# The second warming group ahead of the first turns of g, with a new instruction order: a convolution-and-FFN kernel on one core

## The chip, the cores and the metric

The kernel runs on one core of one Trainium2 chip. The metric is the device time of one execution in microseconds. The core's engines work side by side, each through its own list of instructions in order: TensorE (PE, matrix products), VectorE (DVE), ScalarE (ACT), GpSimd (POOL), and SyncE (SP), which issues DMA transfers. They wait for each other through semaphores. Some transfers are issued by ACT and POOL too. PE writes its results to PSUM, of which this kernel uses four tiles (`ps`), and DVE or ACT copy them out.

## What is computed

Two layers follow each other on 2048 positions of width 640: a long convolution with gates (H3), then a SwiGLU feed-forward network (FFN).

```python
def _A_ref(q, k, v, shift_k, ssm_k, ssm_D):
    ...                      # k_shift: four shifted copies of k times taps shift_k, added
    kv = k_shift * v
    ...                      # y: causal convolution of kv with ssm_k along the sequence, by FFT
    y = y + kv * ssm_D[None, None, :]
    return q * y

def _B_ref(x, w_gate, w_up, w_down):
    g = _silu(x @ w_gate)
    u = x @ w_up
    return (g * u) @ w_down

x = A_q
h = x + _A_ref(_layernorm(x, axis=-1), A_k, A_v, A_shift_k, A_ssm_k, A_ssm_D)
h2 = h + _B_ref(_layernorm(h, axis=-1), B_w_gate, B_w_up, B_w_down)
return h2
```

All inputs and the output are bfloat16. The FFN is 1728 wide.

## The kernel before

**Tiling.** The sequence is cut into four blocks of 512. In each block the stages are, by the names that the code gives them: `g` turns the block of ssm_k (positions to partitions; "turn" is a transpose, on PE against an identity, or by DMA), `G` is its spectrum (products with the cosine table WF, line 347), `k` makes kv from k, v and the taps (line 565, with a table `diag` of taps on diagonals), `X` is the spectrum of kv, `m` multiplies spectra and adds them up (lines 601 to 620: DVE products and sums, of which some sums are done by an adding DMA that POOL issues, line 255), `n` and `i` are the norm's statistics and the inverse transform (lines 677 to 742, products at 725), `t` normalises the result and turns it into `hT`, and `f` is the FFN: gate and up products (line 829), the SiLU and copies on ACT (818, 820), their product on DVE (823), and the down product (886). f of one block stands in the order beside the convolution of the next.

**The first microseconds.** SP issues the loads of ssm_k (g), k, the table WF, q (x), and so on; ACT issues the load of the taps (line 916); POOL issues that of the D row (961) and makes the identity (917). PE runs two warming groups (line 927), 18 and 16 products of ones that nobody reads, and between them, in the order of the code, four small products that turn the taps (934). DVE copies the taps (938), and DVE and POOL fill `diag` (945). Each block of g has four turns of five products (line 426), each copied out of PSUM (428); D's row is added to the first (430). For k the same stands at lines 528 and 532.

**What sets the order.** Every operation is recorded once with a number, an engine, what it reads and writes, and the operations it depends on (`deps`). `ORDER` is a list of these numbers; the program is written out in that order, so each engine gets its operations as they stand there. A number n below zero means operation ~n (46 for -47) in its other form, mostly the other engine: a copy on DVE instead of ACT, a fill of `diag` on POOL instead of DVE, a sum by DMA, a weight load issued by POOL instead of SP. Tiles are handed out along the order too, so the buffer numbers change with it. `schedule` refuses an order in which an operation stands ahead of one that it depends on.

**The dependences that matter here.** The turns of the taps depend on the first warming group, the second warming group on the turns of the taps, and the turns of k (`turned_k`) on the second warming group (`spun`, argument `behind`). The turns of g depend on g and the identity alone.

Of the kernel before, what the change touches and what calls it, by code (L numbers as in the profile page):

```python
# [41 lines left out]
TW = PAD + BLK  # L42
CUTS = ("X0", "G0", "m", "i")
ORDER = [
# [40 lines left out]
SLOTS = {'S': 8, 'big': 13, 'kT': 0, 'tT': 1, 'row': 5, 'sg': 0, 'co': 2, 'ps': 4, 'sm': 6}  # L85
HOME = {t: "big" for t in ("scr", "x", "ld", "t4", "hT", "wgu", "diag")} | {"o": "row", "ps_c": "ps", "ps_f": "ps"}
SPLIT = ((0,), (1,))
# [101 lines left out]
def kernel(ctx: ExitStack, tc: tile.TileContext, A_q, A_k, A_v, A_shift_k, A_ssm_k, A_ssm_D, B_x,  # L189
# [19 lines left out]
    def new(tag):  # L209
        return Buf(HOME.get(tag, tag), None, tag)  # L210
# [4 lines left out]
    def fixed(shp, dt, name):  # L215
        return Buf(None, const.tile(shp, dt, name=name))
# [7 lines left out]
    def pe(ns, fn, r, w, holds=(), late=338):  # L224
        op = plan.add("pe", ns, fn, r, w, holds)
        op.late = late
        return op
# [49 lines left out]
    ident = fixed([P, P], BF16, "ident")  # L277
# [127 lines left out]
            dve(wide(1490, ws), hi4, [odd, (dst, bits((0,), ws=ws))], [(dst, bits((1,), ws=ws))])  # L405
            sum_into(1490, lo4, lambda: ap(dst)[:, 0], lambda odd=odd: ap(odd), [odd], [(dst, bits((0,)))])

    def g_turned(g, drow=None):
        gT = new("t4")
        if plan.block in GTURN:  # L410
            by_r = new("scr")
            act(2350, lambda: nc.scalar.copy(ap(by_r).rearrange("q a b -> q (a b)").rearrange("q (r c p) -> q r c p", r=R, c=KT),
                                             ap(g).rearrange("q (c p r) -> q r c p", c=KT, r=R)), [g], [by_r], [gT])
            for r in range(R):
                def turned_by(q, r=r):
                    return lambda: q.dma_start(out=ap(gT)[:, r, :].rearrange("p (c q) -> p c q", c=KT),
                                               in_=ap(by_r).rearrange("q a b -> q (a b)")[:, r * D:(r + 1) * D], transpose=True)
                transfer(MB / 4, turned_by(nc.sync), [by_r], [(gT, r)])
            return gT
        for r in range(R):  # L420
            pt = conv_ps()

            def tr(r=r, pt=pt):
                src = ap(g).rearrange("q (c p r) -> q c p r", c=KT, r=R)
                for c in range(KT):
                    nc.tensor.transpose(turned(pt)[:, c * P:(c + 1) * P], src[:, c, :, r], ap(ident))  # L426
            pe(285, tr, [g, ident], [pt], [gT], 258)
            evict(lambda copy, r=r, pt=pt: copy(ap(gT)[:, r, :], turned(pt)[:, 0:D]), [pt], [(gT, r)], other=490)
        if drow:
            dve(480, lambda: nc.vector.tensor_add(ap(gT)[0:1, 0, :], ap(gT)[0:1, 0, :], ap(drow)[0:1, :]), [drow], [(gT, 0)])  # L430
        return gT
# [497 lines left out]
    spun = spin(WARMUP[0])  # L929
    pt = new("ps_c")  # L930
# [5 lines left out]
    spun = spin(WARMUP[1])  # L936
# [21 lines left out]
    g = load_g(0)  # L958
    first("Ld")
    drow = new("row")  # L960
# [5 lines left out]
    turned_k(k, spun, table)  # L966
    kv = kv_of(0, v)
    first("g0")
    gT = g_turned(g, drow)
    first("X0")  # L970
    X = [spectrum(kv, "X0", split("X0"))]
    first("G0")
# [12 lines left out]
    for j in range(1, NB):  # L985
# [3 lines left out]
        g = load_g(j)  # L989
# [12 lines left out]
        gT = g_turned(g)  # L1002
# [69 lines left out]
```

## Time and profile before

| what | us |
| --- | --- |
| median of three runs (lowest, highest) | 259.57 (258.88, 260.34) |
| the profiled execution's own time | 260.01 |
| its span, from the first to the last instruction | 258.3 |
| PE, DVE, ACT and POOL busy | 249.9, 193.4, 167.6, 54.6 |
| 540 products of line 829 (gate, up), busy | 120.3 |
| 416 products of line 886 (down), busy | 60.1 |
| 240 products of line 347 (spectra), busy | 38.7 |

An engine is busy while an instruction of its own runs. In the lists of waits a row reads "engine, line, waited for: us in total, times, longest". In the chain of work each row has its start, its length and the work that the end of the kernel hung on at that time. A row of the timeline has start, length, engine, line, operation, output and inputs, how many instructions were merged into it, and in brackets the idle time ahead of it and what ended it.

### The profile page before, as it was taken

How to read it: one execution, taken by the hardware profiler on the slowest of the kernel's cores; microseconds unless marked ns; L12 is line 12 of the kernel's file. 1: busy time of each engine (PE TensorE's matmuls, PEld its weight loads, DVE VectorE, ACT ScalarE, POOL GpSimd, SP SyncE). 2: the span in 40 equal slices, each digit the busy share in tenths (PEclk: the TensorE clock that was granted, in tenths of full speed). 3: DMA queues.
4: the chain of work that ended last, by engine and by line, in shares of the span. 5: the costliest groups of instructions: out<-in, count | busy, mean ns of one | idle time of the engine just before them, and what ended most of it. 6: DMA issues, size and time to landing. Idle time of an engine off the chain costs nothing.

```text
span 258.3 us, 5214 instructions
## 1 busy us (share of the span) xinstructions
PE 249.9 (97%) x2102; PEld 150.9 (58%) x2102; DVE 193.4 (75%) x306; ACT 167.6 (65%) x286; POOL 54.6 (21%) x70
## 2 busy tenths in 40 slices
PE   4999999999999999999999999999999999999994
PEld 3876777854545577744455577544447764444672
DVE  0599999999999899999998999998899300012222
ACT  2599999999898996765876783353497234434400
POOL 2750120122300211044431511039300022000000
PEclk9999999999999999999999999999999999999999
DMA  6993899999979598989999785658990336000003
GB/s 202 404 346 87 223 224 140 296 240 252 190 159 336 171 153 165 168 143 268 204 215 193 115 237 108 129 101 175 223 236 5 63 59 84 0 0 3 0 0 102
DMA packets 48034, 41.45 MB, mean 160 GB/s; under 512 B 25445, under 2 KB 41514, under 8 KB 48010
## 3 DMA queue, kind: packets, MB, share of 16 engines
q1 hardware_dynamic: 40368, 24.57, 36.4%
q0 software_dynamic: 7632, 16.55, 33.8%
q8 instruction: 16, 0.26, 0.4%
q14 instruction: 8, 0.07, 0.1%
q10 hardware_dynamic: 10, 0.01, 0.0%
HBM read 21.94 MB, written 4.59 MB: 103 GB/s over the span
## 4 chain that ended last, share of the span: by engine, by line
PE 74%; DVE 12%; DMA 6%; ACT 4%; issue 2%; POOL 1%; DVEq 0%; POOLq 0%
PE ps L829 35%; PE ps L886 18%; PE ps L347 9%; PE ps L725 5%; PE ps L565 4%; DVE big L607 4%; DMA S<-big 4%; ACT S L339 4%; DMA big<-in_A_ssm_k_dram 2%; DVE S L610 2%; PE ps L426 1%; PE ps L927 1%; DVE big L677 1%; DVE S L680 1%; DVE S L401 1%
## 5 line engine op out<-in xcount | busy, mean ns | idle before, releaser
L829 PE MATMUL ps<-big,big 128*128 128x512 bf16 x540 | 120.3, 379 | 0.0
L829 PEld LDWEIGHTS <-big 128*128 128x128 bf16 x540 | 52.5, 98 | 60.0
L886 PE MATMUL ps<-wd,tT 128*128 128x320 bf16 (+2 forms) x416 | 60.1, 299 | 0.0
L886 PEld LDWEIGHTS <-tT 128*128 128x128 bf16 x416 | 40.6, 98 | 16.4 <-DVE tT L823 0.3
L823 DVE TENSOR_TENSOR tT<-tT,co 128x2048 bf16<-128x2048 bf16 x12 | 14.6, 1221 | 37.8 <-ACT tT L820 29.1
L818 ACT CAST co<-ps 128x1024 bf16<-128x1024 f32 x24 | 24.3, 1011 | 25.5 <-PE ps L829 25.4
L347 PE MATMUL ps<-big,WF 128*128 128x320 bf16 x240 | 38.7, 299 | 0.6 <-ACT co L818 0.3
L607 DVE TENSOR_TENSOR big<-S,S 128x2560 bf16<-128x2560 bf16 x24 | 35.2, 1483 | 0.4 <-DMA out_dram<-big 0.4
L339 ACT ACTIVATE S<-ps 128x640 bf16<-128x640 f32 (+1 forms) x57 | 31.0, 624 | 1.6 <-PE ps L347 1.5
L820 ACT ACTIVATE tT<-ps 128x1024 bf16<-128x1024 f32 x24 | 24.5, 1024 | 10.5 <-PE ps L829 10.2
L347 PEld LDWEIGHTS <-WF 128*128 128x128 bf16 x240 | 22.7, 97 | 12.3 <-issue 1.4
L623 ACT ACTIVATE row<-big 128x640 bf16<-128x640 bf16 x32 | 23.5, 738 | 1.2 <-DVE sm L638 0.7
L610 DVE TENSOR_TENSOR S<-S,big 128x2560 bf16<-128x2560 bf16 x15 | 22.3, 1487 | 0.1
L255 POOL DMA_DIRECT2D S<-big x9 | 11.4, 1267 | 48.0 <-PE ps L347 13.1
L665 ACT ACTIVATE row<-big,sm 128x640 bf16<-128x640 bf16 x21 | 18.3, 917 | 4.9 <-DVE sm L648 2.9
L893 POOL DMA_DIRECT2D out_dram<-row x12 | 13.1, 1481 | 28.6 <-ACT row L892 28.6
L892 ACT CAST row<-ps 128x640 bf16<-128x640 f32 x12 | 7.9, 696 | 14.1 <-PE ps L886 12.2
L739 DVE SCALAR_TENSOR_TENSOR row<-row,ps 128x640 bf16<-128x640 bf16 x16 | 12.8, 816 | 2.5 <-PE ps L725 1.9
L565 PEld LDWEIGHTS <-T 64*128 64x128 bf16 x640 | 11.6, 110 | 3.6 <-issue 3.0
L255 POOL DMA_DIRECT2D S<-S x5 | 6.2, 1243 | 34.5 <-ACT S L339 28.4
L565 PE MATMUL ps<-diag,T 64*128 64x64 bf16 x640 | 13.0, 194 | 0.1
L725 PEld LDWEIGHTS <-WI 128*128 128x128 bf16 x96 | 9.2, 98 | 5.1 <-DVE S L698 0.8
(89 smaller groups left out, 260.7 us busy)
## 6 DMA issues: line engine op xcount, KB each, us to landing
S<-big POOLq DMA_DIRECT2D x9, 640.0 KB, 6.2
S<-S POOLq DMA_DIRECT2D x5, 640.0 KB, 8.0
big<-in_A_ssm_k_dram SPq DMA_DIRECT2D x4, 640.0 KB, 5.9
big<-in_A_q_dram SPq DMA_DIRECT2D x4, 640.0 KB, 7.1
big<-in_A_v_dram SPq DMA_DIRECT2D x4, 640.0 KB, 7.7
big<-in_B_w_gate_dram SPq DMA_DIRECT2D x8, 320.0 KB, 4.8
big<-in_B_w_up_dram POOLq DMA_DIRECT2D x8, 320.0 KB, 7.3
wd<-in_B_w_down_dram SPq DMA_DIRECT2D x1, 2080.0 KB, 12.9
```

The lines of the kernel that those rows point to most:

```text
L339: plan.add("act", 700 if n else 430, lambda: nc.scalar.activation(dst(), src(), ACT.Copy, scale=by), [ps], [part], (), ("dve", 820 if n el ...
L347: nc.tensor.matmul(ap(ps)[:, h, 0:NH], ap(WF)[:, r, c, :], ap(src)[:, r, h * NH:(h + 1) * NH], start=(first and i == 0), stop=(last and i ...
L565: nc.tensor.matmul(out()[:, b, c, :], k, ap(diag)[at, c, t, :], start=(t == 0), stop=(t == 3))
L607: dve(1490, lambda b=b, xs=xs, hs=hs: nc.vector.tensor_mul(flat2(b), X.part(xs), H.part(hs)), [X.at(xs), H.at(hs)], [b], [A.b])
L610: f(A.part(dst), A.part(dst), flat2(b))
L623: act(825, lambda r=r, junk=junk: nc.scalar.activation(ap(junk), ap(x)[:, r, :], ACT.Square, scale=D ** -0.5, accum_out=sm(s, 1)[:, r:r + ...
L665: nc.scalar.activation(ap(row), ap(x)[:, r, :], ACT.Identity, bias=sm(s, 5)[:, r:r + 1], scale=sm(s, 4)[:, r:r + 1])
L725: nc.tensor.matmul(ap(ps)[:, w, 0:NH], m, src[:, w * NH:(w + 1) * NH], start=(i == 0), stop=(i == len(terms) - 1))
L818: act(1010, lambda ps=ps: nc.scalar.copy(ap(co)[:, at:at + 2, :], ap(ps)), src, [(co, gi % 2)])
L820: act(1010, lambda ps=ps: nc.scalar.activation(ap(tT)[:, c:c + 2, :], ap(ps), ACT.Silu), src, [done(range(c, c + 2), ROWS)])
L829: nc.tensor.matmul(ap(ps)[:, i, :], ap(w)[:, k, off:off + P], ap(hT)[:, k, :], start=(k == 0), stop=(k == KT - 1))
L886: nc.tensor.matmul(ap(ps)[:, hf, to:to + n], t, ap(wd)[:, c, col + (hf - hs[0]) * NH:col + (hf - hs[0]) * NH + n], start=(c == order[0]), ...
```

## The change

`g_turned` takes a third argument. For the first block it is the second warming group, and each of the four turns of g gets it as a dependence; nothing else of the program's operations changes. The list `ORDER` is replaced as a whole (959 numbers before and after). Lines behind the change are two further down (L426 becomes L426 still, L428 becomes L430, L927 becomes L929, L677 becomes L679).

```diff
@@ -42,46 +42,46 @@
 ORDER = [
-    0, 20, 2, 4, 14, 21, 45, -47, 1, 49, 5, -51, 19, 47, 3, 51, 7, 6, 52, 29, 53, 8, 9, 48, 17, 201, 25, -27, 30, 23, 18,
+    21, 0, 20, 2, 1, 14, 4, 5, 6, 7, 19, 3, 47, 45, 51, 46, 48, 49, 53, 17, -51, 8, 27, 52, 29, 28, -31, 25, 201, 23, -27,
...
@@ -405,7 +405,7 @@
-    def g_turned(g, drow=None):
+    def g_turned(g, drow=None, behind=None):
         gT = new("t4")
@@ -424,7 +424,9 @@
-            pe(285, tr, [g, ident], [pt], [gT], 258)
+            op = pe(285, tr, [g, ident], [pt], [gT], 258)
+            if behind:
+                op.deps.add(behind)
@@ -966,7 +968,7 @@
     first("g0")
-    gT = g_turned(g, drow)
+    gT = g_turned(g, drow, spun)
```

**The head of PE's list.** Before, from the end of the first warming group; big_72 is the load of g, row_87 the taps, big_73 the load of k, and a name in brackets is what the instruction waits for (DMAHW: a load). Rows that repeat with other buffers are left out.

```order
L927 MATMUL ps_93<-const-bfloat16-1.0 128x128
L426 LDWEIGHTS big_72 [waits DMAHW1_49]
L426 MATMUL ps_94<-ident,big_72 128x128 [waits Pool_49]
...
L934 LDWEIGHTS row_87 [waits DMAHW0_49]
L934 MATMUL ps_96<-ident,row_87 128x5
...
L927 LDWEIGHTS const-bfloat16-1.0
L927 MATMUL ps_95<-const-bfloat16-1.0 128x128 [waits DVE_49]
...
L528 LDWEIGHTS big_73 [waits DMAHW2_49]
L528 MATMUL ps_96<-ident,big_73 128x128 [waits DVE_49]
```

The same place of the changed kernel:

```order
L929 MATMUL ps_93<-const-bfloat16-1.0 128x128
L936 LDWEIGHTS row_87 [waits DMAHW0_49]
L936 MATMUL ps_94<-ident,row_87 128x5 [waits Pool_49]
...
L929 LDWEIGHTS const-bfloat16-1.0
L929 MATMUL ps_95<-const-bfloat16-1.0 128x128
...
L426 LDWEIGHTS big_72 [waits DMAHW1_49]
L426 MATMUL ps_96<-ident,big_72 128x128
...
L530 LDWEIGHTS big_73 [waits DMAHW2_49]
L530 MATMUL ps_93<-ident,big_73 128x128 [waits Activation_49]
```

The turns of the taps and the second warming group have moved ahead of the first instruction that waits for g; behind it stand the turns of g and then those of k.

**The head of DVE's list**, before, from the identity on (big_74 is the turned g, row_86 the D row, T the turned k):

```order
L914 MEMSET ident 128x128
L428 COPY big_74<-ps_94 128x640 [waits PE_49]
L428 COPY big_74<-ps_95 128x640 [waits PE_49]
L938 COPY taps<-ps_96 128x20 [waits PE_49]
L430 TENSOR_TENSOR big_74<-big_74,row_86 1x640 [waits DMASW0_49,DVE_49]
L945 TENSOR_SCALAR diag<-row_88,taps 128x64 [waits DVE_49,Pool_49]
L945 TENSOR_SCALAR diag<-row_88,taps 128x64 x3
L532 COPY T<-ps_95 128x5x128 [waits PE_49]
L532 COPY T<-ps_94 128x5x128 [waits PE_49,Activation_49]
```

And of the changed kernel:

```order
L916 MEMSET ident 128x128
L940 COPY taps<-ps_94 128x20 [waits PE_49]
L432 TENSOR_TENSOR big_74<-big_74,row_86 1x640 [waits DMASW0_49,Activation_49]
L430 COPY big_74<-ps_94 128x640 [waits PE_49]
L534 COPY T<-ps_96 128x5x128 [waits PE_49,Activation_49]
L534 COPY T<-ps_94 128x5x128 [waits PE_49]
L534 COPY T<-ps_95 128x5x128 [waits PE_49,Activation_49]
```

The copy of the taps is first now, the four fills of `diag` have left DVE for POOL, three of g's four copies are ACT's, and the addition of the D row stands ahead of DVE's copy of g.

**The last block's sums and inverse**, on DVE, before: the products and sums of m3 (L607, L610, into S_68), the last gate-times-up products of f2 that stand among them (L823), and the beginning of the inverse (L677, L680, L698, L713).

```order
L610 TENSOR_TENSOR S_68<-S_68,big_77 128x2x1280
L607 TENSOR_TENSOR big_76<-S_71,S_64 128x2560
L646 SCALAR_TENSOR_TENSOR sm_97<-sm_97 128x4
L823 TENSOR_TENSOR tT_85<-tT_85,co_91 128x2048
L610 TENSOR_TENSOR S_68<-S_68,big_76 128x2x1280
L647 SCALAR_TENSOR_TENSOR sm_97<-sm_97 128x4
L823 TENSOR_TENSOR tT_85<-tT_85,co_92 128x2048
L610 TENSOR_TENSOR S_68<-S_68,big_84 128x2x1280
L677 TENSOR_TENSOR big_83<-S_68 128x2560
L680 TENSOR_TENSOR S_68<-S_68 128x2560
L648 TENSOR_TENSOR sm_97<-sm_97 128x4
L698 TENSOR_TENSOR S_68<-S_68 128x1280 x2
```

And of the changed kernel:

```order
L609 TENSOR_TENSOR big_76<-S_71,S_64 128x2560
L825 TENSOR_TENSOR tT_85<-tT_85,co_91 128x2048
L612 TENSOR_TENSOR S_68<-S_68,big_84 128x2x1280
L612 TENSOR_TENSOR S_68<-S_68,big_76 128x2x1280
L650 TENSOR_TENSOR sm_97<-sm_97 128x4
L679 TENSOR_TENSOR big_83<-S_68 128x2560
L682 TENSOR_TENSOR S_68<-S_68 128x2560
L700 TENSOR_TENSOR S_68<-S_68 128x1280 x2
L664 TENSOR_SCALAR row_86<-big_72,sm_97 128x640
L825 TENSOR_TENSOR tT_85<-tT_85,co_91 128x2048
L715 TENSOR_TENSOR S_68<-big_83 128x2x640
```

One gate-times-up product has moved behind the inverse's first sums. On POOL, the adding transfers of this block stand so in the changed kernel (S_71 is X3, S_68 the sum over spectra):

```order
L255 DMA S_68<-big_81 128x2x1280
L255 DMA S_71<-big_83 128x2x1280
L895 DMA out_dram<-row_90 128x640
L255 DMA S_68<-big_83 128x2x1280
L255 DMA S_68<-big_80 128x2x1280
L895 DMA out_dram<-row_87 128x640
```

X3's last sum and one of the m2 sums are transfers now that DVE did before, and two that were transfers are DVE's.

78 rows, old and new, of the table ORDER are left out of this document.

## The prediction

> **What bounds the kernel now.** I read the page's engine line first, then its slices, PE's waits, the chain of work, and last the timeline at the two ends.
>
> ```profile
> span 258.3 us, 5214 instructions
> PE 249.9 (97%) x2102; PEld 150.9 (58%) x2102; DVE 193.4 (75%) x306; ACT 167.6 (65%) x286; POOL 54.6 (21%) x70
> DVE  0599999999999899999998999998899300012222
> ```
>
> PE is busy for 97% of the span. VectorE (DVE) is full too, but only until about slice 30 (some 190 us); in the last quarter it mostly waits. The list of what PE itself waited for is short:
>
> ```profile
> PE ps L426 <- DMA big<-in_A_ssm_k_dram: 3.0, 1, 3.0
> PE ps L927 <- PEq L1056: 0.8, 1, 0.8
> PE ps L347 <- ACT co L818: 0.3, 1, 0.3
> PE ps L725 <- DVE S L698: 0.3, 1, 0.3
> PE ps L347 <- ACT S L339: 0.2, 1, 0.2
> PE ps L426 <- ACT S L339: 0.2, 1, 0.2
> ```
>
> One wait matters: 3.0 us before the first turns of g (L426), for the load of ssm_k. All later ones add up to 1.0. So the kernel is a PE stream that begins in earnest at 5.88 us and runs almost without a hole to 255, and what is taken off that stream shortens the time nearly one for one, as long as DVE keeps ahead. The chain of work (start, us, what) shows the stream's head:
>
> ```profile
> 0.80 5.04 DMA big<-in_A_ssm_k_dram
> 5.88 1.26 PE ps L426 x10
> 7.14 0.22 PE ps L934 x4
> 7.36 1.19 PE ps L426 x10
> 8.55 1.71 PE ps L927 x16
> 10.26 1.36 PE ps L528 x20
> 11.65 3.90 PE ps L347 x26
> ```
>
> Behind the load stand ten turns, the taps products (L934), ten turns, the second warming group (L927, 16 products whose result nobody reads), the turns of k (L528), then the first real products (L347). The taps and the warming group are 0.22 + 1.71 = 1.93 us that need nothing of the awaited load.
>
> **The rate of PE in these first us.** The granted clock reads 1.00 in every row, so it does not tell; the counts in short windows (us, PE busy with its count, clock, DMA) do:
>
> ```profile
> 0.84:2.76 1.92, 1.92 (x18) 1.00 0.22 60
> 8.35:10.05 1.70, 1.70 (x18) 1.00 1.01 393
> 10.65:11.45 0.80, 0.80 (x17) 1.00 1.15 402
> ```
>
> The first window holds 18 products in 1.92 us, 107 ns each; the warming group's 16 in 1.71 us are also 107. After 10.65 it is 17 in 0.80, 47 ns each with the two cut by the window's edges counted whole; L347's 26 products of 320 columns in 3.90 us make 60 per 128 columns. I take 107 ns slow and 56 ns fast, between these. So PE was slow until about 10.65, which is 4.8 us after it began to work without a hole. Whoever works at the slow rate loses half of that time.
>
> **Part 1: the two pieces moved into the hole.** Do the taps land soon enough? The window 0 to 1.9 us of the DMA view holds one queue only, with these packets, and that is the taps load (issued on ACT's queue at 0.80):
>
> ```profile
> q10 hardware_dynamic: 10, 0.01, 0.9%
> row<-in_A_shift_k_dram ACTq DMA_DIRECT2D x1, 5.0 KB
> ```
>
> So they are there at about 1.9, before the first warming group ends at 2.76. They also need the identity, which POOL now makes behind the issue of the D row (0.68 us): at about 1.9 instead of 1.4, still early. Hence taps products 2.8 to 3.0 and warming group 3.0 to 4.7, inside a hole that lasts to 5.88. The cover is 1.2 us wide; were it gone, each us would count in full. What leaves the stream is 0.22 + 1.71 = 1.93 us at the slow rate, worth 1.0 us if the moment at which PE becomes fast stays at 10.65 (a slow us less before that moment is half a fast one, plus the short wait before 11.65).
>
> **Part 2: what is late next.** Turns of g start at 5.88 as before. The next loads (issues, KB, us to landing):
>
> ```profile
> 1.33 0.51 SPq L504 DMA_DIRECT2D big<-in_A_k_dram x1
> 1.89 0.42 SPq L956 DMA_DIRECT2D WF<-const_wf  x1
> big<-in_A_k_dram SPq DMA_DIRECT2D x1, 640.0 KB, 6.2
> WF<-const_wf SPq DMA_DIRECT2D x1, 512.0 KB, 6.9
> ```
>
> k lands at 1.33 + 6.2 = 7.5, the table WF at 1.89 + 6.9 = 8.8; SP issues both as before. At the fast rate g's 20 turns end at 7.0, k's run from 7.5 to 8.6. Then the copies out of PSUM decide:
>
> ```profile
> 6.65 1.03 DVE L428 COPY big<-ps 128x640 bf16<-128x640 bf16 x2 [5.58 <-PE ps L426]
> 7.67 0.47 DVE L430 TENSOR_TENSOR big<-big,row 1x640 bf16<-1x640 bf16 x1
> 8.59 1.29 ACT L428 COPY big<-ps 128x640 bf16<-128x640 bf16 x2 [5.69 <-PE ps L426]
> 10.82 1.54 ACT L532 COPY T<-ps 128x640 bf16<-128x640 bf16 x2 [0.95 <-PE ps L528]
> ```
>
> ACT now has three copies of g (0.65 each) and one of k (0.77): from 6.4 to 9.2. DVE has the D row's addition first (it waits for ACT's first copy and for the D row; a copy of g and three of k are queued behind it), then 0.48 and 3 x 0.45: from 7.5 to about 9.8. The first product of L347 needs a PSUM tile that ACT frees at 9.2. So L347 can start at 9.2 to 9.5 against 11.65: **2.2 to 2.4 us earlier** if PE is fast by then; I take 2.2. If it stays slow to 10.65, 40 turns end at 10.2 and 0.45 us of slow products follow: 1.0 + 0.2 = **1.2 us**. Nothing removes more than the hole itself, 3.0.
>
> Which? Before, 2.1 us of products up to 2.9 did not raise the rate (turns at 5.88 still take 107), and 4.8 without a hole did. After, PE works from 0.84 to 4.7, 3.8 us, then rests 1.2. By the nearer row (4.8) the rise comes during or soon after g's turns, so I lean to it, with two chances in three. The Trainium skill (TensorE: Matmul & The Clock Gate, Part 1) says the gate opens after one busy window of about 3.4 us whose place is free-running; by that rule 3.8 us can but need not hold a whole window, and the sum would be 2.2 in one run and 1.2 in the next. The trace's 4.8 us agrees with a start between 3.4 and 6.8.
>
> **Part 3: the fills of diag and the first kv.**
>
> ```profile
> 7.95 6.81 POOL L945 TENSOR_SCALAR diag<-row,taps 128x64 bf16<-128x64 bf16 x16 [5.44 <-DVE taps L938]
> 8.07 0.67 DVE L945 TENSOR_SCALAR diag<-row,taps 128x64 bf16<-128x64 bf16 x4
> 16.66 0.76 PE L565 MATMUL ps<-diag,T 64*128 64x64 bf16 x40
> ```
>
> POOL takes all 20 fills instead of 16: 20 x 0.43 = 8.6 us, but from 3.5 instead of 7.95, so it ends at 12.2 instead of 14.8. L565 is wanted at 16.66 - 2.2 = 14.4: hidden. DVE loses 0.67.
>
> **Part 4: the rest of the order.** PE has the same instructions. Its stages stand in the same sequence, so it can gain or lose only by new waits, and the place to look is the last block, where DVE and PE meet:
>
> ```profile
> 186.90 1.49 DVE L677 TENSOR_TENSOR big<-S 128x2560 bf16<-128x2560 bf16 x1 [0.82 <-DMA S<-big]
> 190.84 0.72 PE L725 MATMUL ps<-S,WI 128*128 128x320 bf16 x4 [0.28 <-DVE S L698]
> 201.21 0.16 DVE L648 TENSOR_TENSOR sm<-sm 128x4 f32<-128x4 f32 x1
> 202.42 5.16 SPq L756 DMA_TRANSPOSE big<-row  x4
> big<-row SPq DMA_TRANSPOSE x12, 2.6
> 210.56 28.06 PE ps L829 x130
> ```
>
> DVE was 0.28 us late for L725. The statistics end at 201.37, four transposes are issued until 207.58 (1.2 each, so the last at 206.4) and land 2.6 later, 209.0; PE takes up the result at 210.4. The slack is 1.4. PE will come 2.2 earlier and reaches L725 one product group (1.08) later in its order, and f3 at the same place. DVE must therefore be about 1.1 earlier at L725 and 0.8 earlier at the transposes. It starts earlier by the shift of the head itself. Of its instructions up to L677, by the order and the rows' durations: -0.67 (diag), +0.45 and -0.48 (copies), +0.96 (two row sums back from POOL), -0.33, -0.44, -0.33 (two products, one normalisation to ACT), -1.49 and +1.49 (one sum to POOL, another back) = -0.84; and one L823 of 1.22 us moves behind it. Behind L677, the added L823 and a few others cost 0.9 on DVE, and ACT does three of the last four normalisations in a row. Sum: DVE is about 2 us ahead of need at L725 and 1 to 1.5 at the transposes: **0**, bounded by 0 and 1.5 us.
>
> Two large sums of this block (X3's last one and one of X2's products, m2) now go by POOL, and two others came back to DVE. Such a transfer takes
>
> ```profile
> S<-S POOLq DMA_DIRECT2D x5, 640.0 KB, 8.0
> S<-big POOLq DMA_DIRECT2D x9, 640.0 KB, 6.2
> 175.75 11.04 DMA S<-big
> ```
>
> 6.2 to 8.0 us, once 11.0. Between the new one (X3's last sum) and its first reader stand six DVE instructions of 1.4, 8.4 us; between the m2 sum and its reader five, 7.0. At the medians both are just covered; at 11.0 they cost 2.6 and 4.0 on DVE. I take 0.2 for all new waits on PE.
>
> **Sum.** Own time of the profiled execution 260.01 (span 258.3 + 1.7 around it): 260.0 - 2.2 + 0.2 = 258.0. That execution lies 0.44 above the median of the three runs (259.57), within their spread of 1.5; by the median it would be 257.6. I forecast **257.7**.
>
> **Rivals.** (a) The rate rises no earlier: 260.0 - 1.2 + 0.2 = 259.0, by the median 258.6. For it: 3.8 us of work is less than 4.8, and the rest of 1.2 lies in between.
> (b) The new order gives the gain back: the m2 or X3 sum takes 11 us, DVE loses 2.6 to 4.0, all its slack and then PE's at L725 or f3: 259.5 to 260. For it: one in nine S<-big took 11; against it: PE waited only 1.0 us in all behind the head.
> (c) Slower: turns do not raise the rate. Before, 16 warming products stood among the turns and the rate rose 0.6 us behind them; after, 40 turns in a row follow the rest at 4.7. If a turn is no work to whatever grants the rate, PE enters L347 at 10.2 slow and stays so for another 3.4 to 4.8 us, of which half is lost: 1.7 to 2.4 against a lead of 1.45, so 260.3 to 261.0. It decides if the rate has not risen by 4.7. Against it: the first group's 18 products (1.9 us) did not raise it alone, and 16 are fewer, so the turns around them must have counted. The Trainium skill (TensorE: Matmul & The Clock Gate, Part 4) says that transposes do not count as PE work in the same way, which is this rival; by the rows the rate rose within a stretch that was half turns.
> That the change does not do what it says would show as a hole of 3 us; the order of PE's rows excludes it unless the taps land late, which q10 excludes.
>
> **How the numbers follow.** Forecast 0.50 (257.0 to 258.4), (a) 0.22, (b) 0.16, (c) 0.12. A difference of 0.5% (1.3 us, below 258.3 or above 260.9) is about what a measurement of this kernel can tell from no change. Faster: nearly all of the forecast and a third of (a), 0.57; slower: most of (c) and the far end of (b), 0.12; the rest, 0.31, same. The range goes from 256.4 (all of the hole, 3.0) to 260.2, and leaves out most of (c).
>
> **What would show it.** Taps products and second warming group between 2.8 and 4.7; turns of g at 5.88 with 56 ns spacing (forecast) or 107 (a); L347's first product at 9.2 to 9.6 (forecast) or 10.3; the first L829 of the last block at 208 to 208.5 without a wait of PE above 0.5. I am wrong if PE shows new waits above 1 us behind 20 us, or if L347 begins slow behind 10.5 (c).

## The result, and the profile after

| | us, median (lowest, highest) | runs |
| --- | --- | --- |
| before | 259.64 (258.64, 260.34) | 20 |
| after | 258.39 (257.58, 259.44) | 20 |

The ratio is 0.9949, 95% interval 0.9935 to 0.9964: **1.25 us less, 0.5%**. The two profiled executions differ by more, 260.01 against 257.87, or 2.1. Both facts have to be explained: where 2.1 comes from, and why only 1.25 of it is left in the medians.

The changed kernel's engine line, and the list of what PE waited for (engine, line, waited for: us in total, times, longest):

```profile
span 256.2 us, 5180 instructions
PE 247.3 (97%) x2086; PEld 149.1 (58%) x2102; DVE 194.1 (76%) x302; ACT 168.8 (66%) x289; POOL 49.6 (19%) x67
```

```profile
PE ps L426 <- DMA big<-in_A_ssm_k_dram: 1.2, 1, 1.2
PE ps L929 <- PEq L1058: 0.8, 1, 0.8
PE ps L765 <- DVE big L767: 0.6, 1, 0.6
PE ps L426 <- ACT S L339: 0.5, 1, 0.5
PE ps L530 <- DMA big<-in_A_k_dram: 0.4, 1, 0.4
PE ps L347 <- ACT co L820: 0.3, 1, 0.3
...
```

The hole before the first turns has gone from 3.0 to 1.2. Two waits inside the kernel are new or larger: 0.6 at L765 (the turns of the normalised rows) and 0.5 at L426 in place of 0.2. The timeline of the head (start, length, engine, line, count, and in brackets the idle time ahead and what ended it):

```profile
0.84 2.08 PE L929 MATMUL ps<-const-bfloat16-1.0 128*128 128x128 bf16 x18 [0.84 <-PEq L1058]
...
3.04 0.20 PEld L936 LDWEIGHTS <-row 5*128 5x128 bf16 x4 [0.39 <-DMA row<-in_A_shift_k_dram]
3.04 0.29 PE L936 MATMUL ps<-ident,row 5*128 5x5 bf16 x4
...
3.26 1.45 PE L929 MATMUL ps<-const-bfloat16-1.0 128*128 128x128 bf16 x16
...
3.73 8.42 POOL L947 TENSOR_SCALAR diag<-row,taps 128x64 bf16<-128x64 bf16 x20 [0.89 <-DVE taps L940]
...
5.93 1.31 PE L426 MATMUL ps<-ident,big 128*128 128x128 bf16 x20 [1.22 <-DMA big<-in_A_ssm_k_dram]
...
7.55 0.57 DVE L432 TENSOR_TENSOR big<-big,row 1x640 bf16<-1x640 bf16 x1 [4.01 <-DMA row<-in_A_ssm_D_dram]
...
7.68 1.61 PE L530 MATMUL ps<-ident,big 128*128 128x128 bf16 x20 [0.44 <-DMA big<-in_A_k_dram]
...
9.26 4.21 PE L347 MATMUL ps<-big,WF 128*128 128x320 bf16 x28
```

Taps and second group now lie in the hole. The group's 16 products take 1.45 us instead of 1.71, and the 20 turns of g 1.31, where ten took 1.26 before: the rate has risen during the group (the trace's record of the granted clock, a list of stretches, starts the one at full rate at 4.05 us, against 10.65 before). L347 starts at 9.26 instead of 11.65, a lead of 2.39.

How that lead fares, by the first start of three groups in the timelines:

| first start, us | before | after | lead |
| --- | --- | --- | --- |
| spectra, L347 | 11.65 | 9.26 | 2.39 |
| f0's gate, L829/L831 | 52.75 | 50.77 | 1.98 |
| f3's gate, L829/L831 | 210.40 | 208.12 | 2.28 |
| last product's end | 254.91 | 252.63 | 2.28 |

The middle costs 0.4, and the last block gives 0.3 back, since DVE is no longer late for the inverse's products (the wait of 0.3 at L725 is gone).

### The profile page after: what moved, and what is told of

The parts are those of the page before. It is cut to its first block, busy times and chain, and to the rows that moved or that the text cites. A ratio compares the mean times of both kernels' runs of the same rounds, so it can differ in the third digit from the quotient of the medians.

```text
span 256.2 us, 5180 instructions
## 1 busy us (share of the span) xinstructions
PE 247.3 (97%) x2086; PEld 149.1 (58%) x2102; DVE 194.1 (76%) x302; ACT 168.8 (66%) x289; POOL 49.6 (19%) x67
## 3 DMA queue, kind: packets, MB, share of 16 engines
HBM read 21.94 MB, written 4.59 MB: 104 GB/s over the span
## 4 chain that ended last, share of the span: by engine, by line
PE 90%; ACT 3%; DMA 2%; DVE 2%; issue 1%; DVEq 0%; POOLq 0%
PE ps L831 45%; PE ps L888 24%; PE ps L347 10%; PE ps L727 5%; PE ps L567 4%; ACT S L339 3%; DMA row<-in_A_ssm_D_dram 2%; PE ps L426 1%; DVE tT L825 0%; DVE big L767 0%; PE ps L765 0%; DVE S L340 0%; PE ps L530 0%; DVE big L432 0%; DVE row L905 0%
## 5 line engine op out<-in xcount | busy, mean ns | idle before, releaser
L831 PE MATMUL ps<-big,big 128*128 128x512 bf16 x524 | 118.5, 379 | 0.9 <-issue 0.2
L831 PEld LDWEIGHTS <-big 128*128 128x128 bf16 x540 | 52.4, 98 | 60.4
L347 PE MATMUL ps<-big,WF 128*128 128x320 bf16 x240 | 38.3, 299 | 0.3 <-ACT co L820 0.3
L339 ACT ACTIVATE S<-ps 128x640 bf16<-128x640 f32 (+1 forms) x57 | 31.6, 619 | 4.1 <-PE ps L347 4.0
L347 PEld LDWEIGHTS <-WF 128*128 128x128 bf16 x240 | 22.9, 97 | 11.3 <-issue 1.6
L255 POOL DMA_DIRECT2D S<-big x9 | 10.9, 1208 | 82.7 <-DVE sm L644 28.3
L612 DVE TENSOR_TENSOR S<-S,big 128x2560 bf16<-128x2560 bf16 x16 | 23.7, 1486 | 0.2
L667 ACT ACTIVATE row<-big,sm 128x640 bf16<-128x640 bf16 x22 | 19.5, 918 | 3.1 <-DVE sm L650 3.1
L567 PEld LDWEIGHTS <-T 64*128 64x128 bf16 x640 | 11.3, 110 | 3.5 <-issue 3.0
L567 PE MATMUL ps<-diag,T 64*128 64x64 bf16 x640 | 12.6, 194 | 0.0
L588 DVE TENSOR_TENSOR big<-S,S 128x2560 bf16<-128x2560 bf16 (+1 forms) x10 | 12.2, 1218 | 0.0
```

What stands on the lines that cost most here:

```text
L255: nc.gpsimd.dma_start(out=to(), in_=what(), accum_op=ALU.add, max_dma_last_dim=2 * D * 2)
L339: plan.add("act", 700 if n else 430, lambda: nc.scalar.activation(dst(), src(), ACT.Copy, scale=by), [ps], [part], (), ("dve", 820 if n el ...
L347: nc.tensor.matmul(ap(ps)[:, h, 0:NH], ap(WF)[:, r, c, :], ap(src)[:, r, h * NH:(h + 1) * NH], start=(first and i == 0), stop=(last and i ...
L567: nc.tensor.matmul(out()[:, b, c, :], k, ap(diag)[at, c, t, :], start=(t == 0), stop=(t == 3))
L612: f(A.part(dst), A.part(dst), flat2(b))
L667: nc.scalar.activation(ap(row), ap(x)[:, r, :], ACT.Identity, bias=sm(s, 5)[:, r:r + 1], scale=sm(s, 4)[:, r:r + 1])
```

## The experiments

The ratios are to the kernel before, on the same chip; "after" is the 258.39 above.

**1. Head alone, and the rest of the order alone.** The first kernel has the new dependence and otherwise the order of before, with only four numbers moved at its start (1 is the taps' load, 5 to 7 are the taps products, the second group and the copy of the taps); the second has the old dependences, PE's head as before, and the new order behind it.

```diff
 # head alone: the new dependence of the turns of g, and
-    0, 20, 2, 4, 14, 21, 45, -47, 1, 49, 5, -51, 19, 47, 3, 51, 7, 6, 52, 29, 53, 8, 9, ...
+    0, 20, 2, 1, 4, 5, 6, 7, 14, 21, 45, -47, 49, -51, 19, 47, 3, 51, 52, 29, 53, 8, 9, ...
 # rest alone: no new dependence, and
-    21, 0, 20, 2, 1, 14, 4, 5, 6, 7, 19, 3, 47, 45, 51, 46, 48, 49, 53, 17, -51, 8, ...
+    21, 0, 20, 2, 1, 14, 4, 19, 3, 47, 45, 5, 7, 46, 51, 48, 49, 53, -51, 6, 17, 8, ...
```

> The order of before, with only the taps' products, their copy and the second warming group moved ahead of the first turns of g (and the dependence). Theory (the gain is the head's: the hole is filled, and in a part of the executions PE gets fast earlier): 258.0 to 258.7, the first product of L347 at 9.3 to 10.4 instead of 11.65. Rival (the gain comes from the new order of all the rest): 259.6, as before, with the lead of the head lost again behind it in waits of PE of 1 us or more.

> The new order everywhere, but at PE's head the taps and the second warming group stand among and behind the turns of g, as before. Theory (head alone): 259.2 to 259.9, with the hole of 3 us back. Rival (the rest of the order): 258.4.

Head alone: 257.38 (257.1 to 258.29, 6 runs), ratio 0.9923 [0.9899, 0.9947], a gain of 2.2. Rest alone: 259.71 (259.53 to 260.69, 12 runs), ratio 1.0009 [0.9994, 1.0023]. The head brings everything, and more than the theory's 258.0 to 258.7. The new order behind it brings nothing by itself, and together they are 1.0 worse than the head alone by the medians, 0.7 by the ratios, whose intervals overlap. The profile of the rest alone shows what the new order does: L347 starts 0.82 earlier than before (10.83; the rate rose at 9.15 there), but PE then waits 0.6 for DVE at the turns of the normalised rows, and 0.41 of the lead is left at f0's gate (52.34 against 52.75).

**2. Which part of the head: filling the hole, or the earlier rate?** Three kernels change the second group in the changed kernel: down to one product, up to 30, and (later, after the first result) 16 of which 15 are cut to 1x1. A fourth cuts the group in the same way in the head-alone kernel.

```diff
-WARMUP = (18, 16)
+WARMUP = (18, 1)        # or (18, 30)
 # the cut group
-            for _ in range(n):
-                nc.tensor.matmul(ap(warm)[:, 0, 0:P], ones, ones, start=True, stop=True)
+            for i in range(n):
+                m = 1 if short and i else P
+                nc.tensor.matmul(ap(warm)[0:m, 0, 0:m], ones[:, 0:m], ones[:, 0:m], start=True, stop=True)
```

> The changed kernel with one product instead of 16 in the second warming group. Theory (the group in the hole is what gets PE fast by the first turns in about half of the executions; turns count as work, so it gets fast some 4.8 us behind 5.9 at the latest): turns of g and k at 107 ns, L347 from 10.3, 258.8 to 259.4 in nearly every execution, 0.4 to 1.0 above the changed kernel. Rival (turns do not count): L347 starts slow at 10.3 and stays so to 13.6 or later, 260.3 or more. Rival (the group does nothing): 258.4, as the changed kernel.

> The changed kernel with 30 products in the second warming group, so that PE works without a rest from 0.84 to the first turn. Theory (what sets the fast and the late executions apart is whether the 3.8 us of work at the head cover a whole period of whatever grants the rate): PE is fast before 5.9 in nearly all executions, the group then ends inside the hole, 257.6 to 258.0 with a spread under 1 us. Rival (the length of the work does not matter): the spread stays at 1.9 us and the slow ones lose 0.6 more, 258.5 to 259.0.

> The changed kernel, with fifteen of the second group's sixteen warming products cut to 1x1 (same number of instructions on TensorE, hardly any work before the turns). Theory (the group's work is worth only the earlier rise of the rate; what the kernel without the group lost beyond that, 1.50 and 0.83 and 0.61 us in the L567 bursts with no releaser, comes from instruction packets that land elsewhere in the program): turns of g 107 ns apart, rise near 11, first L347 near 10.1 to 10.3, no wait at L567 without a releaser, and 259.0 to 259.4, 0.6 to 1.0 above the changed kernel's 258.4. Rival (the stalls belong to a late rate, not to the count of instructions): the same stalls at 20 and 37 us and 261.4 to 262. Rival two (the rate does not matter): 258.4.

> The new head alone on the old order (257.38), with the second group's fifteen products cut to 1x1. Theory (the gain of the head is the hole's 1.0 to 1.2 that needs no rate, plus about 1.0 from the earlier rise): 258.3 to 258.7, first L347 near 10.1. Rival (filling the hole is all of it): 257.4. Rival two (the rise is all of it): 259.5.

| kernel | us (runs) | ratio | rate rises | first L347 |
| --- | --- | --- | --- | --- |
| after | 258.39 (20) | 0.9949 [0.9935, 0.9964] | 4.05 | 9.26 |
| head alone | 257.38 (6) | 0.9923 [0.9899, 0.9947] | 4.59 | 9.08 |
| after, group of 1 | 261.77 (6) | 1.0088 [1.0064, 1.0113] | 10.95 | 10.08 |
| after, group of 30 | 258.69 (12) | 0.9972 [0.9954, 0.9989] | 5.20 | 9.09 |
| after, 15 of 16 cut | 258.96 (10) | 0.9971 [0.9953, 0.9989] | 11.25 | 10.05 |
| head alone, 15 of 16 cut | 258.41 (10) | 0.9951 [0.9936, 0.9966] | 10.89 | 9.93 |

The last row against head alone is the clean one: filling the hole without the rate brings 259.57 - 258.41 = 1.2, the earlier rise another 258.41 - 257.38 = **1.0** by the medians. By the ratios the second step is 0.7, and the two intervals overlap at their ends; the head with a group of 24 (257.40, in experiment 3), run on the same chip as the cut group, gives 1.0 again. In the changed kernel the same cut costs only 0.6, which fits that it has the early rise in about half of its executions (experiment 3). The group of 30 has the early rise in its profile too, but sits 0.3 above the changed kernel. My theory for it (257.6 to 258.0, spread under 1 us) failed: 11 of its 12 runs lie within 0.8 us, one at 260.45, and the median is in the range of the rival; its PE waits 0.4 us for a transposing load of k near 30 us, which the changed kernel's does not. That wasn't followed further.

The group of 1 had a surprise: slower than before by 0.9%, in the time range of the rival that turns don't count, though the rate rose only 0.3 later than before and L347 started 1.6 earlier. Its PE waits and the place of the longest, in the timeline:

```profile
PE ps L567 <- issue: 2.9, 3, 1.5
```

```profile
18.01 0.58 PE L567 MATMUL ps<-diag,T 64*128 64x64 bf16 x28
20.10 0.94 PE L567 MATMUL ps<-diag,T 64*128 64x64 bf16 x52 [1.50 <-issue]
```

PE stops in the middle of 80 short products and waits for nothing that the trace shows. The same place with the cut group, which has as many PE instructions as the changed kernel but does as little before the turns:

```profile
18.15 1.34 PE L567 MATMUL ps<-diag,T 64*128 64x64 bf16 x80
```

No stop, and no wait of L567 "issue" in that kernel's list; 2.8 us less in the median. So the stops hang on how many instructions stand ahead, not on the rate and not on the missing work. Counted in the trace, PE has 449, 961 and 1473 instructions behind it (products, weight loads and its sequencer's) when it stops: the distance is 512 both times. That points to the supply of instructions; the rest is argued from times only: the queue of instruction packets (16 of 16 KB) shows one at 17.64, 34.47 and 50.28 in the group-of-1 kernel, landed 1.2 to 1.4 us before PE goes on at each of the three stops (20.10, 36.97, 52.8), and one more between each stop and the next. In the kernel with the cut group the first of these packets has landed at 16.43, 1.7 us before that burst begins. Why it comes later here is open.

**3. Why half of the executions are slower.** The 20 times of the changed kernel fall into nine at 257.58 to 257.95, eight at 258.39 to 258.59 and three at 259.04 to 259.44. In all profiles the clock record's stretches at full rate have lengths of 72, 73 or 74 times 3.413 us: the rate is decided on a grid of 3.413 us that starts anywhere. For a profile one can list boundaries at which the rate did not rise, or the first at which it did, with PE's idle time in the 3.413 us ahead of it:

| kernel | boundary, us | idle ahead of it | rose |
| --- | --- | --- | --- |
| after | 4.05 | 0.3 | yes |
| head alone | 4.59 | 0.0 | yes |
| head alone, fills on POOL (exp. 5) | 7.10 | 0.4 | yes |
| both repairs (exp. 4) | 3.55 | 0.7 | no, at 10.38 |
| the same profile | 6.96 | 0.8 | no, at 10.38 |
| zero fill early (exp. 4) | 5.85 | 0.8 | no, at 9.26 |
| addition behind (exp. 4) | 6.08 | 0.9 | no, at 9.50 |

PE's rest ahead of the turns in "fills on POOL" (boundary 7.10) and "both repairs" (6.96):

```profile
5.90 1.85 PE L426 MATMUL ps<-ident,big 128*128 128x128 bf16 x20 [0.41 <-DMA big<-in_A_ssm_k_dram]
```

```profile
5.76 2.32 PE L426 MATMUL ps<-ident,big 128*128 128x128 bf16 x20 [0.79 <-DMA big<-in_A_ssm_k_dram]
```

So a window with 12% idle (0.41 us) still raises the rate, and those with 20% (0.70) and more do not. (The head alone with the cut group did not rise at 4.07 with 0.45 idle either, but some 0.6 us of its work there were products of 1x1.) In the changed kernel PE works from 0.84 to 5.1 when the rate is late (the group then takes 1.89 us), and rests to 5.9. A boundary raises the rate there if it lies between 4.0 and 5.4 (with at most 0.4 us idle) or, at the utmost, between 3.7 and 5.7 (at most 0.7): 1.4 to 2.0 of 3.41, an estimate of 41 to 59% of the executions. At the other places of the grid the rate rises at 7.1 us or later. Nine in 20 is 45%.

The times of single runs agree. A run's mean granted clock is below 1 when the rate falls behind the last product but inside the span, and how far below tells where it falls, and thereby the grid. The nine low runs all have 1.000; eight of the eleven others have 0.997 to 0.999, and their falls, carried back along the grid, belong to boundaries at about 6.0 to 7.4 us (a step of 0.001 is 0.5 us here), where the rise is late. It costs 258.48 - 257.72 = 0.76, the difference of the medians of the two larger clusters. The three others (258.44, 258.50 and 259.44, at 1.000) are not placed by this, and what sets the three highest apart isn't shown. Nor was an execution of the changed kernel with a late rise profiled; the nearest is the kernel with the addition behind (experiment 4), which rises at 9.50 and took 258.65.

The Trainium skill (TensorE: Matmul & The Clock Gate, Part 1) states a free-running window of 3413 ns; the 72 to 74 lengths agree.

Would more work close the gap? Head alone, with a group of 24 that ends 0.28 before the turns:

> The new head alone on the old order, with 24 products in the second warming group instead of 16, so that TensorE works almost up to the first turn of g. Theory (the changed kernel's scatter of 257.6 to 259.4 comes from the rate rising in or after the turns in some executions; work without the 1.2 us rest makes it rise before them in all): first turns at 5.7 to 5.9 as before and fast, all runs within 0.5, median 257.0 to 257.4 against 257.38. Rival (scatter comes from elsewhere, or sixteen more instructions move an instruction packet into a burst of short products, as without the group): scatter stays 1 us or more, or the median is 258 and over with waits at L567 that have no releaser.

257.40 (257.26 to 258.3, 6 runs), ratio 0.9921 [0.99, 0.9942]. No gain and the same scatter: the part of the theory that all executions would come together failed. The grid itself allows a rise as late as 7.4 then, and whether that is the remaining scatter isn't shown.

**4. What the new order loses.** In the changed kernel, the timeline about 47 us:

```profile
46.99 1.12 POOL L952 MEMSET wd<- 64x640 bf16 x1
47.07 1.54 DVE L664 TENSOR_SCALAR row<-big,sm 128x640 bf16<-128x640 bf16 x1
...
48.53 0.47 DVE L767 COPY big<-ps 128x640 bf16<-128x640 bf16 x1
...
49.06 0.44 PE L765 MATMUL ps<-ident,row 128*128 128x128 bf16 x5 [0.62 <-DVE big L767]
```

and in the head-alone kernel:

```profile
47.15 0.44 DVE L664 TENSOR_SCALAR row<-big,sm 128x640 bf16<-128x640 bf16 x1
...
47.91 0.48 DVE L767 COPY big<-ps 128x640 bf16<-128x640 bf16 x1
```

DVE's normalisation takes 1.54 instead of 0.44 while POOL fills the last rows of wd (the down product's weights) with zeros, and PE waits 0.62 for the copy behind it. The five other profiles in which that fill stands so late (rest alone, groups of 1 and 30, the cut group, addition behind) have the same row, 1.53 to 1.55 long. Before, that fill stood in the head:

```profile
15.73 0.62 POOL L950 MEMSET wd<- 64x640 bf16 x1
```

The re-searched order has it behind two large transfers of POOL. The second suspect was the D row's addition (L432), which makes DVE wait 4.0 us at the head. Three kernels move the one, the other, and both:

```diff
 # zero fill early: in ORDER, number 16 behind 15
-    ... 66, -44, 63, 15, 67, 44, 58, ...
+    ... 66, -44, 63, 15, 16, 67, 44, 58, ...
-    ... 364, 200, 349, 350, 16, 269, 468, ...
+    ... 364, 200, 349, 350, 269, 468, ...
 # addition behind the copy of g
-    ... 48, 49, 53, 17, -51, 8, ...
+    ... 48, 49, 17, -51, 53, 8, ...
```

> The changed kernel, with one instruction of GpSimd, the zero fill of wd's last rows (L952), moved from behind two large transfers (46.99 us) to right behind the fill of tail (near 12.8 us); nothing else moves. Theory (it ran beside VectorE's L664 at 47.07 and stretched it from 0.44 to 1.54, which made VectorE late for TensorE's L765 by 0.6): L664 0.44, no wait at L765, f0's first gate product near 50.3 instead of 50.77, and 257.8 to 258.1. Rival (VectorE's L664 was slow for another reason, or the delay is taken up by a later wait anyway): L664 stays at 1.5 or the time stays at 258.4.

> The changed kernel, with VectorE's addition of the D row (L432, which waits 4.0 us for a row that lands at 7.45) placed behind its copy of g instead of ahead of it. Theory (VectorE stands idle there but TensorE does not wait for that copy for long: L347's first product at 9.26 waits for VectorE's copies by 0.2 at most): first L347 at 9.0 to 9.1, 258.2 to 258.4. Rival (the addition ahead is what the changed kernel loses against the head alone): L347 near 8.8 and 257.8 or less.

> The changed kernel with the zero fill of wd early (257.87 against 258.39 by itself) and the addition of the D row behind the copy of g. Theory: 257.6 to 257.9, f0's first gate product 0.1 to 0.2 earlier than with the zero fill alone at the same moment of the rate's rise. Rival (the two gains add to what the head alone has): 257.4.

| kernel | us (lowest, highest, runs) | ratio |
| --- | --- | --- |
| zero fill early | 257.87 (257.22, 258.31, 6) | 0.9929 [0.9908, 0.995] |
| addition behind | 258.6 (257.7, 259.4, 7) | 0.9949 [0.993, 0.9968] |
| both | 257.8 (257.13, 258.42, 5) | 0.9911 [0.9891, 0.9931] |

With the zero fill early:

```profile
12.86 0.63 POOL L952 MEMSET wd<- 64x640 bf16 x1
```

```profile
47.67 0.97 DVE L664 TENSOR_SCALAR row<-big,sm 128x640 bf16<-128x640 bf16 x1
```

PE's wait at L765 is gone from its list, and the median is 0.5 lower, as expected (the two intervals overlap, so the 0.5 stands on the vanished wait as much as on the medians). In this profile L347 starts 0.46 later than in the changed kernel's (the rate rose at 9.26), and f0's gate product at 50.79 against 50.77: the 0.46 has been won in between. My expectation of 0.44 for L664 was wrong: 0.97 remain, beside POOL's issue of two transfers. What of POOL's issuing holds DVE up isn't settled; in the head-alone kernel an issue from 46.45 to 47.70 did not. The Trainium skill (SBUF — State Buffer, section SBUF: two separate sides) says that VectorE and GpSimd share a pair of ports, which whoever starts first, GpSimd or a VectorE operation in a mode that uses both ports, holds for its whole instruction. With the zero fill that agrees to 0.1: it ends at 48.11, and 0.44 more is 48.55, against an end of L664 at 48.61.

The addition's place is worth nothing, as the theory had it: 258.6 (0.2 above its range) against 258.39, with the rate late in its profile and L347 at 9.83. Both repairs together can't be told from the zero fill alone: 257.8 against 257.87, and the intervals overlap.

**5. The head alone, improved.** It still has four diag fills on DVE ahead of the copies of k, and PE waits 0.24 for one of these at L347. One number of its order, 9, becomes -10 (the same fill, on POOL).

> The new head alone on the old order, with the last four diag fills (0.73 us on VectorE at 7.90, ahead of its copies of k) on GpSimd too, as the changed kernel has them. Theory (TensorE's wait of 0.24 for VectorE's copy at L347 goes, the fills end near 12.1 and are wanted at 14.0): first L347 at 8.8 to 8.9, 257.1 to 257.4. Rival (GpSimd, now 1.7 us later with the issue of f0's first weights and the zero fill, makes f0 late, or the load of k then decides): 257.4 or above.

257.59 (256.88 to 258.36, 6 runs), ratio 0.9918 [0.9898, 0.9938]. It doesn't help by more than the scatter, which is the rival's outcome (257.4 or above). PE's wait for DVE at L347 is gone from its list. But the profile has the rise at 7.10 and L347 at 9.40, PE came there later by itself, and new are 0.5 for the load of the taps and 0.3 for ACT's copies at L530; so what the fills cost isn't shown.

The lowest median here is that of the new head on the old order, 257.38, 1.0 under the changed kernel and 2.2 under the one before. The same head with 24 products (0.9921) or the fills on POOL (0.9918), and the changed kernel with both repairs (0.9911), can't be told from it (0.9923).

## Why the prediction came out as it did

- **Part 1** (both pieces move into the hole, 1.2 us of cover): nearly as forecast, 3.04 to 4.71 instead of 2.8 to 4.7, and 1.22 are left of the hole. The landing of the taps was misjudged: I took it from one profile of before (1.9), and in the changed kernel their weight load waited for them until 3.04, with the fills on POOL until 3.38. The cover absorbed it, as it did POOL's issue of the D row ahead of the identity.
- **The rate**, 2.2 or 1.2 us: both occur. The profiled execution had 2.39 at L347, and the forecast's place of it (9.2 to 9.6) held. The two-in-three lean to the early rise came from comparing 3.8 us of work with 4.8; the runs put something else in its place, the idle share of a window on a grid. In the changed kernel nine of 20 executions get it. The cut groups priced the two parts at 1.2 without the rate and 1.0 for it; rival (a)'s 1.2 was right to the tenth by the medians. The measured 258.39 is a mixture of the two, nearer to (a)'s 258.6 than to the 257.7 of the forecast.
- **Part 2** (what is late next, L347 at 9.2): right, by an estimate that put DVE's late D row at no cost; moving it changed nothing.
- **Part 3** (diag hidden): right. The fills end at 12.15 and L567 starts at 14.32 without a wait.
- **Part 4** (last block, 0): right; no wait at L727, f3 at 208.12, between 208 and 208.5 as forecast. Neither of the two sums by POOL took part: rival (b)'s place was wrong.
- **0.2 for all new waits** is a term that was too small: the lead lost 0.4 by f0, and the repaired order is 0.5 faster. I looked at the sums on DVE and POOL's transfers in the last block; what cost was a zero fill of 0.62 us that POOL had moved from 15.73 to 46.99, a step that I had not followed at all. Head alone against after is 1.0 in the medians, 0.7 by the ratios; the zero fill makes 0.5 of that. What is left includes the wait at L426 (0.5 instead of 0.2) and how many executions rise early (four of six runs lie in the head alone's lower cluster, against nine of 20); it isn't resolved further.
- **The step to the median.** The sum of 2.0 was right for the profiled execution (2.1). I carried it to the median as if both kernels' profiled executions lay alike in their spread. Before's lies 0.37 above its median, after's 0.52 below: 2.14 - 0.37 - 0.52 = 1.25. The 0.52 is, by experiment 3, the late rise in the other half. That 258.39 lies within the 257.0 to 258.4 of the forecast is partly luck: it does so by 0.01, with a late rise in half of the executions and a zero fill of which the sum knew nothing.
- **Rival (c)** (turns are no work to the rate): refuted by the kernels with next to no group, where the rate rose at 10.9 to 11.3 behind 40 turns and 0.9 to 1.2 us of L347. In 3.413 us up to 10.95 there are 2.5 us of turns; without them 0.9 us of work would have had to do. Cleaner still is the kernel with the zero fill early, whose rate rose at 9.26: in the 3.413 us ahead PE did turns alone (L426 and L530), and L347 began behind it:

  ```profile
  5.87 2.32 PE L426 MATMUL ps<-ident,big 128*128 128x128 bf16 x20 [0.76 <-DMA big<-in_A_ssm_k_dram]
  7.99 1.89 PE L530 MATMUL ps<-ident,big 128*128 128x128 bf16 x20
  9.72 4.39 PE L347 MATMUL ps<-big,WF 128*128 128x320 bf16 x28
  ```

  The Trainium skill (TensorE: Matmul & The Clock Gate, Part 4) says that transposes do not count in the same way; in these runs they counted.

## What to carry to other kernels

Work that needs no input belongs ahead of the first load, and here it paid twice: it left the stream, and it raised PE's rate before the real work; price the two apart by a kernel that fills the hole with products of no size. When an order is searched anew along with a small move, run the move alone on the old order: here it was worth more than both together (2.2 against 1.25 by the medians). In a new order, follow the small steps of GpSimd too, and look which VectorE instruction they then run beside.

## What the runs showed of the hardware

- The rate of PE rises only at boundaries 3.413 us apart, if PE was idle for no more than 0.4 us of the 3.413 before; with 0.7 it did not. Turns count as work: a window with nothing else raised the rate at 9.26.
- PE can stop for 0.6 to 1.5 us in bursts of products of 64 columns (80 in 1.34 us) with no releaser in the trace, here at three places 512 of its instructions apart; 30 instructions more at the head of the program removed the stops: 261.77 against 258.96.
- One DVE instruction of 0.44 us took 1.53 to 1.55 beside a zero fill of POOL, in all six profiles where the two met.
